# Attention stage of a fused attention and two-MoE kernel: scatters spread over chunks, state scaling on ScalarE, a product split over two engines, loads and fills in another order

## The chip, the cores and the metric

One core of a Trainium2 chip runs the whole kernel. The metric is device time in microseconds for one launch. Engines are named as in the profile: PE (TensorE), DVE (VectorE), ACT (ScalarE), POOL (GpSimd) and SP (SyncE, which here issues DMA transfers).

## The reference, cut to what matters

Three computations follow each other: an attention with a decaying state per head, a mixture of eight experts with one expert per token, and a second mixture that some tokens skip.

```python
# attention: B=4, H=8, S=768, D=48
for t in range(S):
    state = alpha[:, :, t, :, None] * state + einsum('bhd,bhe->bhde', k[:, :, t], v[:, :, t])
    y[:, :, t] = einsum('bhd,bhde->bhe', q[:, :, t], state)
x = y.transpose(0, 2, 1, 3).reshape(3072, 384)
# first MoE, E=8, F=1024: e_idx = argmax(x @ w_gate)
for e in range(E):
    out[mask] = gate_w[mask] * eom[mask, e] * (relu(x[mask] @ w1[e]) @ w2[e])
# second MoE: where x @ w_skip > 0, out = x + gate_w * (relu(x @ w1[e]) @ w2[e]); else out = x
```

## The kernel before

Attention works on 24 chunks of 128 time steps (4 batches of 6 chunks, all 8 heads at once as 4 pairs `hp`). Inside a chunk the decay is a running product `P` (`p_scan`, a DVE scan, L878). `p_recip` makes `r` = 1/P on ACT by a logarithm and an exponential. `p_k` makes `t` = P*r on POOL (L904), `r` = k*r on DVE (L911) and `k2` on DVE (L913). The product with t serves a Newton step. `p_q` makes `qp` = q*P on POOL (L922). PE multiplies k2 and qp (`scores`), DVE applies the causal mask to two tiles (`mask`, L941), PE transposes k2 (`k_back`), and ACT copies it out as `kn`. `state` has PE form `pu` from kn and v, and DVE adds the state of the chunk before (L976) and multiplies by the chunk's total decay `ptots` (L977; for the first chunk of a batch one instruction, L974). The last chunk of a batch needs no state. `y_of` forms y on PE; `x_rows` turns it into token rows.

The order is written out by hand. The list `stages` gives each step a lag, so that iteration i of the loop handles chunk i+4 in `p_scan`, chunk i+2 in `p_k` and `p_q`, chunk i in `scores` and `mask`, and chunk i-1 in `state` and `y_of`. Each engine executes its instructions in that program order. A declared dependency holds t back until the scan of the next chunk has ended. Every third iteration SP loads the next half batch of a, k, q (buffers for three halves) and one iteration later the v of a half (three buffers).

Four chunks (512 tokens) make a group. When its rows stand, `x_route` finds the expert of each token (iterations i%4==2 for groups 0 to 3), and one iteration later `x_place` computes the positions and issues four scatters, one per chunk, from POOL (L218) into `scr1`, a region of rows per expert in HBM. Group 4 is placed after the last mask but one, and group 5 is placed in the first expert's stage. `fill_region` (L139) writes empty rows to the head of each expert's region: `scr1` in two parts, of which the second comes at iteration 3, and `scr2` of the second mixture at iteration 16, all through SP. In iterations 7 to 23 with i%3 not 0, half a piece of expert 0's weights is split into a high and a low part (`split_half`, L303 on ACT and L304 on DVE).

After attention, `stream` runs 18 items: first expert 0 (306 rows, then 126 late rows), then experts 1 to 7 with 432 rows each, then the second mixture's experts. While one expert computes, the next expert's six weight pieces are loaded by SP (L292) through three buffers `st` and split. The rows of the first item use two of these buffers.

Of the kernel before, what the change touches and what calls it, by code (L numbers as in the profile page):

```python
# [8 lines left out]
F32 = mybir.dt.float32  # L9
# [4 lines left out]
AF = mybir.ActivationFunctionType  # L14
ALU = mybir.AluOpType
# [4 lines left out]
B, H, S, D = 4, 8, 768, 48  # L20
E, DM, FF = 8, 384, 1024
NT = B * S
C = 128
NCH = S // C
NTILE = NT // C
NP = H // 2
PR = 112
HB = 3
HALF = HB * C
CAP = 3456  # L30
# [7 lines left out]
P2, G2 = 128, 2  # L38
N2 = P2 * G2
GT = 4  # L40
LATE = 1
# [11 lines left out]
def kernel(  # L53
# [17 lines left out]
    nc = tc.nc  # L71
    ctx.enter_context(tc.manual_schedule())

    def pool(stack, name, bufs, space=None, **kw):
        if space is not None:
            kw["space"] = space
        return stack.enter_context(tc.tile_pool(name=name, bufs=bufs, **kw))
# [1 line left out]
    cp = pool(ctx, "const", 1)  # L79
    sp = pool(ctx, "small", 2)  # L80
    wpe = pool(ctx, "wpe", 1)
    rp = pool(ctx, "rows", 2)
    stp = pool(ctx, "stage", 3)
    psM = pool(ctx, "psM", 1, PSUM)
    dp = pool(ctx, "dram", 1, DRAM)
# [1 line left out]
    scr1 = dp.tile([E * CAP + N1, PAY], F32, name="scr1")  # L87
    scr2 = dp.tile([E * CAP + N1, PAY], F32, name="scr2")
# [7 lines left out]
    ecap = cp.tile([1, E], BF16, name="ecap")  # L96
    ecl1 = cp.tile([1, 2, E], BF16, name="ecl1")
# [8 lines left out]
    ptots = cp.tile([PR, NTILE, NP], F32, name="ptots")  # L106
# [30 lines left out]
    def fill_region(scr, pp, gg, e0=0, e1=E):  # L137
        for e in range(e0, e1):
            nc.sync.dma_start(  # L139
                out=scr[e * CAP:e * CAP + pp * gg, :].rearrange("(p g) d -> p g d", p=pp),  # L140
                in_=fill[0:pp, None, :].to_broadcast([pp, gg, PAY]),
            )
# [74 lines left out]
    def scatter(dst, idx, j, src, pp, bound, key=None):  # L217
        ins = nc.gpsimd.indirect_dma_start(  # L218
            out=dst, out_offset=bass.IndirectOffsetOnAxis(ap=idx.bitcast(U32)[0:pp, j:j + 1], axis=0),
            in_=src, in_offset=None, bounds_check=bound, oob_is_err=False,  # L220
        )
        if key is not None:
            if groups[key]:
                tc.declare_no_dep(ins.ins, group=key, reason="the rows differ")
            tc.add_to_no_dep_group(key, ins.ins)
            groups[key].append(ins)
# [19 lines left out]
        nc.vector.tensor_reduce(out=ls, in_=lo, axis=AX.X, op=ALU.add)  # L246
        return dl, ex, oh, ls

    def place_tokens(xrow, sm_ps, routed, row, key=None):
        dl, ex, oh, ls = routed  # L250
        psr = sm_ps[:, 256:256 + GT * E]
        rank_mm(128, GT, oh, ohs1, row, psr)
        em = sp.tile([128, GT], F32, name="em")
        nc.scalar.activation(out=em, in_=ls, func=AF.Exp, scale=-1.0)
        sm = exp_sum(128, GT, exps(128, GT, dl, "a") if ex is None else ex, "a")
        pos = sp.tile([128, GT], F32, name="posa")
        positions(128, GT, oh, psr, pos, "a")
        dn = sp.tile([128, GT], F32, name="dn")
        nc.vector.scalar_tensor_tensor(out=dn, in0=em, scalar=1.0, in1=sm, op0=ALU.add, op1=ALU.mult)
        pi = sp.tile([128, GT], I32, name="pi")  # L260
        nc.vector.tensor_copy(pi, pos)
        nc.vector.reciprocal(out=xrow[:, :, 384], in_=dn)
        count(128, GT, oh, ohs1, "a")
        for j in range(GT):
            scatter(scr1[:, :], pi, j, xrow[:, j, :], 128, E * CAP - 1, key)

    def rows_from(xt, pt):
        for hp in range(NP):
# [52 lines left out]
    def open_pools(stack, early=False):  # L321
        nonlocal wpo, mp, psH, psY, psT
        if not early:
            mp = pool(stack, "moe", 1, reuse_waits="tile")
        wpo = pool(stack, "wpo", 1, reuse_waits="tile")
        psH = pool(stack, "psH", 2, PSUM, reuse_waits="tile")
        psY = pool(stack, "psY", 3, PSUM, reuse_waits="tile")
        psT = pool(stack, "psT", 2, PSUM, reuse_waits="tile")
# [518 lines left out]
    with ExitStack() as actx:  # L847
        inp = pool(ictx, "inp", 1)
        wk = pool(actx, "wk", 2, side="right")
# [1 line left out]
        ps1 = pool(actx, "ps1", 1, PSUM)  # L851
        NB_IN = 3
        NQ = 4
        NB_V = 3
        ain = [inp.tile([128, HB, NP, C + 1], F32, name=f"ain{i}") for i in range(NB_IN)]
        kin = [inp.tile([128, HB, NP, C], F32, name=f"kin{i}") for i in range(NB_IN)]
        qin = [inp.tile([128, HB, NP, C], F32, name=f"qin{i}") for i in range(NB_IN)]
# [1 line left out]
        NHALF = 2 * B  # L859
# [7 lines left out]
        def load_v(h):  # L867
            b, u = divmod(h, 2)
            nc.sync.dma_start(out=vin[h % NB_V], in_=vn[b][:, u * HB:(u + 1) * HB])

        P_t, r_t, k_t, q_t, A_t, kn_t, S_t, x_t, xt_t, sm_t, rt_t, lt_t = ({} for _ in range(12))
        scans = {}

        def p_scan(i):
            h, c = divmod(i, HB)
            a = ain[h % NB_IN]
            P = wk.tile([PR, NP, C + 1], F32, name="P", bufs=4)
            scans[i] = nc.vector.tensor_tensor_scan(  # L878
                out=P.rearrange("p a b -> p (a b)"), data0=a[0:PR, c].rearrange("p a b -> p (a b)"),
                data1=floor[0:PR].rearrange("p a b -> p (a b)"), initial=1.0, op0=ALU.mult, op1=ALU.max,  # L880
            )
            P_t[i] = P[:, :, 1:C + 1]

# [34 lines left out]
        def p_q(i):  # L918
            h, c = divmod(i, HB)
            P = P_t[i]  # L920
            qp = wk.tile([PR, NP, C], F32, name="qp", bufs=NQ)
            nc.gpsimd.tensor_tensor(  # L922
                out=qp, in0=qin[h % NB_IN][0:PR, c], in1=P, op=ALU.mult
            )
            q_t[i] = qp
            nc.scalar.activation(out=ptots[:, i], in_=P[:, :, C - 1], func=AF.Copy)
# [34 lines left out]
        def state(i):  # L961
            b, c = divmod(i, NCH)
            if c == NCH - 1:
                return
            v, kn = v_of(i), kn_t.pop(i)
            pu = ps1.tile([PR, NP, D], F32, name="pu")
            for hp in range(NP):
                v0 = 2 * hp * D
                nc.tensor.matmul(pu[0:64, hp], kn[:, hp, 0:64], v[:, v0:v0 + D])
                nc.tensor.matmul(pu[64:PR, hp], kn[:, hp, 64:PR], v[:, v0 + D:v0 + 2 * D])  # L970
            sn = wk.tile([PR, NP, D], F32, name="S", bufs=3)
            pt = ptots[:, i, :, None].to_broadcast([PR, NP, D])
            if c == 0:
                nc.vector.tensor_tensor(out=sn, in0=pu, in1=pt, op=ALU.mult)  # L974
            else:
                nc.vector.tensor_tensor(out=sn, in0=pu, in1=S_t[i - 1], op=ALU.add)  # L976
                nc.vector.tensor_tensor(out=sn, in0=sn, in1=pt, op=ALU.mult)  # L977
            S_t[i] = sn

        def y_of(i):  # L980
# [56 lines left out]
        def x_place(i):  # L1037
            g, j = divmod(i, GT)
            if j == GT - 1:
                place_tokens(x_t.pop(g), sm_t[g], rt_t.pop(g), ecap if g < NTILE // GT - LATE else ecl1, "a")  # L1040

        def among(fn, i0, i1):
            def run(i):
# [6 lines left out]
        x_route_0, x_place_0 = (among(fn, 0, rest) for fn in (x_route, x_place))  # L1050
# [22 lines left out]
        for which, c in (("ak", 0), ("a", 1), ("q", 0), ("kq", 1), ("a", 2)):  # L1073
# [11 lines left out]
        pieces = []  # L1085
        stages = (
            (p_recip, 3), (scores, 0), (mask, 0), (state, -1), (x_route_1, -3), (p_k, 2), (p_q, 2), (k_back, 0),
            (x_place_0, -4), (x_place_1, -3), (x_route_0, -3), (p_scan, 4), (y_of, -1), (x_rows, -2), (p_check, 3),
        )

        def constants(n):
# [13 lines left out]
        for i in range(NTILE + 2):  # L1105
            if i == early_at + 1:
                bump(ohs1, ecl1, sm_t[NTILE // GT - LATE - 1][0:1, 400:401], EARLY1)
            for fn, lag in stages:
                if 0 <= i + lag < NTILE and (fn, i + lag) not in done:
                    fn(i + lag)  # L1110
                if fn is p_scan and 6 <= i < 24 and i % 3:
                    split_half(w_cur, (i - 6) // 3, i % 3 - 1, pieces[(i - 6) // 3])
            if i % HB == 1 and 2 <= (i + 2) // HB < NHALF:
                load_v((i + 2) // HB)
            if i == early_at:
                xe = []
                for g0 in range(0, ITEMS[0][4], 2):
                    g1 = min(g0 + 2, ITEMS[0][4])
                    st = stp.tile([128, 1024], F32, name="st")
                    part = st[:, 0:(g1 - g0) * PAY].rearrange("p (g d) -> p g d", g=g1 - g0)  # L1120
                    load_into(part, ITEMS[0], g0, g1)
                    xe += [part[:, g] for g in range(g1 - g0)]
            if i % HB == 0 and i // HB + 3 < NHALF:
                load_half(i // HB + 3, "akq")
            if i == HB:
                fill_region(scr1, P1, G1, FILL)
            if i == 16:
                fill_region(scr2, P2, G2)
            if 4 <= i and i % 3 == 1 and (i - 4) // 3 < 6:
                pieces.append(load_piece(w1a, w2a, 0, (i - 4) // 3, stp))  # L1130

# [59 lines left out]
            place_tokens(xrow, smp, route_tokens(smp), ecl1)  # L1191

    open_pools(ectx, early=True)
    last = NTILE - 1
    stream(w_cur, "b", "o", (xe, xc, x_first), {
        (0, 0): (lambda: x_route(last),), (0, 2): (lambda: x_place(last),),
# [97 lines left out]
```

## Time and profile before

| what | value |
|---|---|
| time before, median of 3 runs | 605.98 us (602.32 to 607.67) |
| the profiled execution's own time | 606.18 us |
| its span, first to last instruction | 604.5 us |
| PE busy | 558.1 us, 92% of the span |
| DVE busy | 385.7 us, 64% |
| ACT busy | 295.7 us, 49% |
| POOL busy | 179.0 us, 30% |
| mean granted TensorE clock | 0.948 |

The span is the time between the first and the last instruction that the profiler recorded. The busy shares are means over two very different stages, attention and experts.

### The profile page before, as it was taken

The numbers are of one execution on the slowest core, as the hardware profiler recorded it, in microseconds if no ns is written. First come the engines' busy times: TensorE is split into PE (matmuls) and PEld (weight loads), VectorE is DVE, ScalarE is ACT, GpSimd is POOL, SyncE is SP. The second block draws the span as 40 slices with busy tenths as digits, with TensorE's granted clock in tenths as the row PEclk, the third lists the DMA queues.
The fourth block names the chain that finished last, engine by engine and source line by source line (L and its number), as shares of the span: only waits on it lengthen the run. The fifth ranks groups of instructions, "written<-read, shape, count | busy, mean of one in ns | idle before, by whom it ended". The sixth has DMA issues, their size and how long they took to land.

```text
span 604.5 us, 11709 instructions
## 1 busy us (share of the span) xinstructions
PE 558.1 (92%) x4545; PEld 509.0 (84%) x4545; DVE 385.7 (64%) x872; ACT 295.7 (49%) x675; POOL 179.0 (30%) x186
## 2 busy tenths in 40 slices
PE   5895987979789999999999999999999999999995
PEld 3674875867569889999999999999998999999995
DVE  6798696979735546365555555463744777677751
ACT  4565463755334455353544444444544655555640
POOL 4155545455532032023140506060406010011111
PEclk9698878788888999999999999999999999999998
DMA  8999744960133822516171626253345567666620
GB/s 322 360 352 306 299 180 141 346 212 1 54 112 105 249 72 85 186 27 234 41 250 36 221 70 225 72 192 104 100 162 196 171 204 241 210 214 204 218 86 22
DMA packets 34797, 103.98 MB, mean 172 GB/s; under 512 B 6316, under 2 KB 13100, under 8 KB 34732
## 3 DMA queue, kind: packets, MB, share of 16 engines
q1 hardware_dynamic: 27788, 91.18, 45.0%
q0 software_dynamic: 6944, 11.96, 5.7%
q8 instruction: 38, 0.62, 0.5%
q14 instruction: 27, 0.22, 0.1%
HBM read 82.62 MB, written 27.13 MB: 182 GB/s over the span
## 4 chain that ended last, share of the span: by engine, by line
PE 67%; DVE 13%; DMA 10%; POOL 4%; SPq 2%; issue 2%; ACT 1%; POOLq 0%; DVEq 0%; ACTq 0%
PE ph L399 26%; PE py L446 16%; PE py L455 11%; DMA vin<-in_vn_dram 4%; PE py L399 3%; DVE r L911 3%; DVE A L941 3%; DVE P L878 2%; PE pt L355 2%; DMA st<-in_w2a_dram 2%; POOL scr L218 2%; PE pt L485 2%; DMA scr<-fill 2%; PE ph L417 2%; DVE k L913 1%
## 5 line engine op out<-in xcount | busy, mean ns | idle before, releaser
L218 POOL DMA_INDIRECT scr<-x,pi x56 | 67.8, 1210 | 218.9 <-DVE osb L201 133.3
L399 PE MATMUL ph<-xh,w1h 128*128 128x432 f32 (+3 forms) x330 | 110.1, 334 | 0.0
L399 PE MATMUL ph<-xl,w1h 128*128 128x432 f32 (+3 forms) x330 | 106.7, 323 | 0.0
L399 PE MATMUL ph<-xh,w1l 128*128 128x432 f32 (+3 forms) x330 | 106.5, 323 | 0.0
L405 DVE SCALAR_TENSOR_TENSOR hl<-ph,hh 128x432 fp32r<-128x432 f32 (+3 forms) x110 | 56.3, 512 | 69.3 <-ACT hh L404 68.4
L404 ACT ACTIVATE hh<-ph 128x432 fp32r<-128x432 f32 (+3 forms) x110 | 50.1, 455 | 91.0 <-PE ph L399 90.9
L304 DVE TENSOR_TENSOR w2l<-st,w2h 128x512 fp32r<-128x512 f32 x96 | 64.5, 688 | 41.0 <-ACT w2h L303 40.9
L303 ACT ACTIVATE w2h<-st 128x512 fp32r<-128x512 f32 x96 | 58.1, 625 | 47.0 <-DMA st<-in_w2a_dram 25.8
L446 PE MATMUL py<-hh,w2h 128*128 128x432 f32 (+1 forms) x192 | 69.1, 360 | 0.0
L446 PE MATMUL py<-hh,w2l 128*128 128x432 f32 (+1 forms) x192 | 67.5, 351 | 0.0
L446 PE MATMUL py<-hl,w2h 128*128 128x432 f32 (+1 forms) x192 | 67.4, 351 | 0.0
L304 DVE TENSOR_TENSOR w1l<-st,w1h 128x512 fp32r<-128x512 f32 x96 | 63.1, 686 | 4.4 <-ACT w1h L303 2.5
L399 PEld LDWEIGHTS ph<-xh,w1h 128*128 128x128 f32 x330 | 62.8, 190 | 2.7 <-issue 1.6
L399 PEld LDWEIGHTS ph<-xh,w1l 128*128 128x128 f32 x330 | 62.8, 190 | 1.1
L399 PEld LDWEIGHTS ph<-xl,w1h 128*128 128x128 f32 x330 | 62.5, 189 | 1.5
L934 PE MATMUL ps<-qp,k 48*128 48x128 f32 x384 | 37.7, 318 | 22.4 <-DVE A L941 13.5
L303 ACT ACTIVATE w1h<-st 128x512 fp32r<-128x512 f32 x96 | 56.5, 623 | 0.0
L934 PEld LDWEIGHTS ps<-qp,k 48*128 48x128 f32 x384 | 31.1, 215 | 28.3 <-issue 21.7
L218 POOL DMA_INDIRECT out_dram<-ot,ti x16 | 15.6, 976 | 119.6 <-DVE ot L550 109.2
L455 PE MATMUL py<-w2h,hh 128*128 128x384 f32 (+1 forms) x136 | 48.4, 356 | 0.0
L455 PE MATMUL py<-w2l,hh 128*128 128x384 f32 (+1 forms) x136 | 45.9, 337 | 0.0
L455 PE MATMUL py<-w2h,hl 128*128 128x384 f32 (+1 forms) x136 | 43.9, 337 | 0.0
(216 smaller groups left out, 1115.7 us busy)
## 6 DMA issues: line engine op xcount, KB each, us to landing
st<-in_w1a_dram SPq DMA_DIRECT2D x24, 512.0 KB
st<-in_w2a_dram SPq DMA_DIRECT2D x24, 512.0 KB
st<-in_w1b_dram SPq DMA_DIRECT2D x24, 512.0 KB
st<-in_w2b_dram SPq DMA_DIRECT2D x24, 512.0 KB
ain<-in_ad_dram SPq DMA_DIRECT2D x7, 774.0 KB
kin<-in_kd_dram SPq DMA_DIRECT2D x7, 768.0 KB
qin<-in_qd_dram SPq DMA_DIRECT2D x7, 768.0 KB
scr<-fill SPq DMA_DIRECT2D x8, 654.8 KB
```

The source lines that it names most:

```text
L218: ins = nc.gpsimd.indirect_dma_start(out=dst, out_offset=bass.IndirectOffsetOnAxis(ap=idx.bitcast(U32)[0:pp, j:j + 1], axis=0), in_=src, i ...
L303: nc.scalar.activation(out=hi, in_=src, func=AF.Copy)
L304: nc.vector.tensor_tensor(out=lo, in0=src, in1=hi.bitcast(F32), op=ALU.subtract)
L355: nc.tensor.transpose(pt[:, g * pp:(g + 1) * pp], rows_of(xr, g)[0:pp, kb * 128:(kb + 1) * 128], ident[0:pp, 0:pp])
L399: nc.tensor.matmul(ph[:, 0:n], w[:, kb, f * 128:(f + 1) * 128], x[:, kb, 0:n], start=(k == 0), stop=(k == 3 * KB - 1),)
L404: nc.scalar.activation(out=hh[:, f, 0:n], in_=ph[:, 0:n], func=AF.Relu)
L405: nc.vector.scalar_tensor_tensor(out=hl[:, f, 0:n], in0=ph[:, 0:n], scalar=0.0, in1=hh[:, f, 0:n].bitcast(F32), op0=ALU.max, op1=ALU.subtract,
L446: nc.tensor.matmul(py[d], w[:, f, dsl], hx[:, f, 0:pp * gg], start=(f == 0 and k == 0), stop=(f == FB - 1 and k == 2),)
L455: nc.tensor.matmul(py[g], hx[:, f, gsl], w[:, f, :], start=(f == 0 and k == 0), stop=(f == FB - 1 and k == 2),)
L911: nc.vector.tensor_tensor(out=r, in0=kk, in1=r, op=ALU.mult)
L934: nc.tensor.matmul(pss[j][:, hp], k2[rr, hp], qp[rr, hp])
L941: nc.vector.tensor_tensor(out=a, in0=ps, in1=causal[:, None, :].to_broadcast([128, NP, C]), op=ALU.mult)
```

## The change

Six things are changed in the attention stage. The scatters of groups 0 to 3 are collected in a list, and a new step `x_send`, right behind `x_place_0`, issues one of them per iteration; groups 4 and 5 still issue four in a row. The multiplication of the state by `ptots` goes from DVE to ACT, as one scaled copy per head pair (four per chunk). The product qp goes to DVE for chunks with i%4 of 2 or 3 and stays on POOL for the others. The v of a half is loaded at i%3==0 instead of 1, ahead of that iteration's a, k, q, with two buffers instead of three. The second part of scr1's fill is issued at iteration 0 instead of 3. The fill of scr2 is issued after the attention loop, ahead of the expert stage's loads. `P` has three buffers instead of four, and the token rows have three instead of two.

```diff
-    rp = pool(ctx, "rows", 2)
+    rp = pool(ctx, "rows", 3)
...
-    def place_tokens(xrow, sm_ps, routed, row, key=None):
+    def place_tokens(xrow, sm_ps, routed, row, key=None, later=None):
...
         for j in range(GT):
-            scatter(scr1[:, :], pi, j, xrow[:, j, :], 128, E * CAP - 1, key)
+            if later is None:
+                scatter(scr1[:, :], pi, j, xrow[:, j, :], 128, E * CAP - 1, key)
+            else:
+                later.append(lambda j=j: scatter(scr1[:, :], pi, j, xrow[:, j, :], 128, E * CAP - 1, key))
...
-        NB_V = 3
+        NB_V = 2
...
-            P = wk.tile([PR, NP, C + 1], F32, name="P", bufs=4)
+            P = wk.tile([PR, NP, C + 1], F32, name="P", bufs=3)
...
-            nc.gpsimd.tensor_tensor(
+            (nc.gpsimd if i < 2 or i % 4 < 2 else nc.vector).tensor_tensor(
                 out=qp, in0=qin[h % NB_IN][0:PR, c], in1=P, op=ALU.mult
             )
...
-            pt = ptots[:, i, :, None].to_broadcast([PR, NP, D])
-            if c == 0:
-                nc.vector.tensor_tensor(out=sn, in0=pu, in1=pt, op=ALU.mult)
-            else:
+            if c:
                 nc.vector.tensor_tensor(out=sn, in0=pu, in1=S_t[i - 1], op=ALU.add)
-                nc.vector.tensor_tensor(out=sn, in0=sn, in1=pt, op=ALU.mult)
+            for hp in range(NP):
+                nc.scalar.activation(
+                    out=sn[:, hp], in_=(sn if c else pu)[:, hp], func=AF.Copy, scale=ptots[:, i, hp:hp + 1]
+                )
...
+                    to_send if g < NTILE // GT - LATE - 1 else None,
...
+        def x_send(i):
+            if to_send:
+                to_send.pop(0)()
...
-            (x_place_0, -4), (x_place_1, -3), (x_route_0, -3), (p_scan, 4), (y_of, -1), (x_rows, -2), (p_check, 3),
+            (x_place_0, -4), (x_send, 0), (x_place_1, -3), (x_route_0, -3), (p_scan, 4), (y_of, -1), (x_rows, -2), (p_check, 3),
...
-            if i % HB == 1 and 2 <= (i + 2) // HB < NHALF:
-                load_v((i + 2) // HB)
...
+            if i % HB == 0 and NB_V <= i // HB + 1 < NHALF:
+                load_v(i // HB + 1)
             if i % HB == 0 and i // HB + 3 < NHALF:
                 load_half(i // HB + 3, "akq")
-            if i == HB:
+            if i == 0:
                 fill_region(scr1, P1, G1, FILL)
-            if i == 16:
-                fill_region(scr2, P2, G2)
...
     open_pools(ectx, early=True)
+    fill_region(scr2, P2, G2)
```

## Rows read from the trace of the kernel before

**Rows 1.** Windows: busy us and count per engine, granted clock, DMA share, GB/s.

```profile
190.00:600.00 410.00, 405.11 (x2661) 383.25 (x2660) 241.43 (x602) 200.94 (x428) 92.21 (x84) 1.00 0.47 152
81.70:88.30 6.60, 6.60 (x87) 5.40 (x87) 6.33 (x15) 4.11 (x11) 2.59 (x3) 0.79 0.92 383
132.00:137.50 5.50, 4.31 (x27) 3.77 (x29) 5.43 (x9) 3.72 (x11) 2.61 (x3) 0.53 0.01 3
```

**Rows 2.** Timeline of DVE: start, duration, instruction; one iteration, then part of the next.

```profile
44.94 1.23 DVE L878 TENSOR_TENSOR_SCAN P<-ain,floor 112x516 f32<-112x516 f32 x1
46.09 1.26 DVE L941 TENSOR_TENSOR A<-ps,causal 128x512 f32<-128x512 f32 x2
...
47.65 1.24 DVE L977 TENSOR_TENSOR S<-S,ptots 112x192 f32<-112x192 f32 x1
48.81 0.68 DVE L911 TENSOR_TENSOR r<-kin,r 112x512 f32<-112x512 f32 x1
...
50.13 1.23 DVE L878 TENSOR_TENSOR_SCAN P<-ain,floor 112x516 f32<-112x516 f32 x1
51.27 1.26 DVE L941 TENSOR_TENSOR A<-ps,causal 128x512 f32<-128x512 f32 x2
52.75 1.65 DVE L911 TENSOR_TENSOR r<-kin,r 112x512 f32<-112x512 f32 x1 [0.21 <-POOL t L904]
```

**Rows 3.** Timeline of DVE around a group's four scatters.

```profile
93.58 1.23 DVE L878 TENSOR_TENSOR_SCAN P<-ain,floor 112x516 f32<-112x516 f32 x1
94.73 0.67 DVE L304 TENSOR_TENSOR w1l<-st,w1h 128x512 fp32r<-128x512 f32 x1
...
101.39 1.66 DVE L911 TENSOR_TENSOR r<-kin,r 112x512 f32<-112x512 f32 x1 [4.80 <-POOL t L904]
...
128.33 1.66 DVE L911 TENSOR_TENSOR r<-kin,r 112x512 f32<-112x512 f32 x1 [3.02 <-POOL t L904]
```

**Rows 4.** Timeline of POOL in the same stretch.

```profile
76.26 1.46 POOL L904 TENSOR_TENSOR t<-P,r 112x512 f32<-112x512 f32 x1 [2.60 <-DVE P L878]
...
93.66 2.65 POOL L218 DMA_INDIRECT scr<-x,pi  x1 [2.72 <-DVE osa L201]
96.61 0.98 POOL L218 DMA_INDIRECT scr<-x,pi  x1 [0.30 <-DVE A L941]
...
100.16 1.19 POOL L904 TENSOR_TENSOR t<-P,r 112x512 f32<-112x512 f32 x1
```

**Rows 5.** DVE's waits, 0 to 185 us: total, times, longest.

```profile
DVE r L911 <- POOL t L904: 16.4, 5, 4.8
...
DVE S L974 <- PE pu L970: 2.8, 1, 2.8
```

**Rows 6.** Timeline of SP's DMA issues, 40 to 180 us.

```profile
40.01 8.10 SPq L139 DMA_DIRECT2D scr<-fill  x4
...
105.77 9.81 SPq L139 DMA_DIRECT2D scr<-fill  x8
...
175.14 0.68 SPq L336 DMA_DIRECT2D st<-scr  x2
175.93 8.01 SPq L292 DMA_DIRECT2D st<-in_w1a_dram  x3
```

**Rows 7.** Timeline of ACT: two short instructions, and expert 1's first split.

```profile
89.41 0.19 ACT L926 ACTIVATE ptots<-P 112x4 f32<-112x4 f32 x1
89.50 0.19 ACT L254 ACTIVATE em<-ls 128x4 f32<-128x4 f32 x1
...
193.46 0.63 ACT L303 ACTIVATE w1h<-st 128x512 fp32r<-128x512 f32 x1
```

**Rows 8.** Timeline of PE: two chunks' scores back to back, and scores after an idle stretch.

```profile
113.60 1.16 PE L934 MATMUL ps<-qp,k 48*128 48x128 f32 x16
...
118.72 1.16 PE L934 MATMUL ps<-qp,k 48*128 48x128 f32 x16
...
133.19 2.58 PE L934 MATMUL ps<-qp,k 48*128 48x128 f32 x16 [3.29 <-DVE A L941]
```

More of the change, by code (lines that the diff above doesn't have):

```diff
@@ L871 @@
         P_t, r_t, k_t, q_t, A_t, kn_t, S_t, x_t, xt_t, sm_t, rt_t, lt_t = ({} for _ in range(12))
-        scans = {}
+        scans, to_send = {}, []
         def p_scan(i):
@@ L1039, in x_place @@
             if j == GT - 1:
-                place_tokens(x_t.pop(g), sm_t[g], rt_t.pop(g), ecap if g < NTILE // GT - LATE else ecl1, "a")
+                place_tokens(
+                    x_t.pop(g), sm_t[g], rt_t.pop(g), ecap if g < NTILE // GT - LATE else ecl1, "a",
+                    to_send if g < NTILE // GT - LATE - 1 else None,
+                )
+        def x_send(i):
+            if to_send:
+                to_send.pop(0)()
         def among(fn, i0, i1):
```

## The prediction

> **What bounds the kernel now.** I read the stages first, as windows. From 190 to 600 us PE is busy for 405 of 410 us at granted clock 1.00 [rows 1]. The change issues almost nothing there. So what it can win lies in the attention stage, the first 185 us, where DVE is busy nearly throughout (6.33 of 6.60 us in one window [rows 1]), and whatever moves the end of that stage moves the end of the kernel by as much, because the experts start when attention's last rows are there.
>
> Inside attention I followed DVE in its timeline, from scan to scan. A plain iteration takes 5.19 us (44.94 to 50.13) without idle time: scan, two masks and the state's addition (46.09 to 47.65), its multiplication, r, k2 [rows 2]. Where a group has just been placed it is another thing: from the scan at 93.58 until r is done at 103.05 go 9.5 us, against 4.6 (44.94 to 49.49) in the plain one, because DVE waits 4.80 us for t [rows 2, 3]. POOL's timeline explains it: four scatters come one behind the other from 93.66, and t starts only at 100.16, though the scan that it must keep clear of ended at 94.8 [rows 3, 4]. DVE waited 16.4 us for t in five waits [rows 5]; 0.21 of them stand in rows 2, so 16.2 lie behind the four groups of scatters. One more stall is DVE's 2.8 us for pu [rows 5], at the first state of the third half: v comes late there, since SP issued it behind the second part of scr1's fill, which held SP for 8.10 us [rows 6].
>
> The sum is made against the profiled execution, 606.18 us with a span of 604.5; it lies 0.2 above the median of the runs, 605.98, so a difference carries over. About 1% (6 us) is what a measurement of this kernel can tell from no change.
>
> **Scatters, one per iteration.** A scatter behind the first costs POOL 0.98 plus 0.30, 1.28 us [rows 4]. Three of them leave the path ahead of t: 3.84 us per group, but no more than DVE waited, 3.02 at one of the four [rows 3]. Together 3 x 3.84 + 3.0 = 14.5 us. What is late next: the first scatter stays, 2.65 us long, so t starts at 96.6 instead of 95 and DVE still waits some 1 us. The 12 scatters that move land on POOL behind t or qp of later iterations, where POOL waited for the next scan anyway, for 2.60 us in a row of that kind [rows 4]. A scatter of 1.28 disappears in that; one that stretches like the first (2.65 + 0.30) exceeds it by 0.35. So the bounds are 13 (a third of those 12 pay 0.35) and 16 (all the waits of rows 5 go). I take 14.5.
>
> **State scaled by ACT.** This takes 1.16 us (47.65 to 48.81) off DVE in a plain iteration [rows 2]. That is not what is won. The iteration that follows in rows 2 has no state at all, yet from its masks until r is done it takes 3.13 us (51.27 to 54.40) against 3.40 (46.09 to 49.49): r now comes early, first waits for t and then runs beside qp on POOL, 1.65 us instead of 0.68. So where qp stays on POOL about 0.3 us is won per iteration. The Trainium skill's page "SBUF — State Buffer", section "Who interferes with whom", has a rule for it: a DVE instruction with two SBUF inputs contends with a GpSimd instruction that reads SBUF, and whichever issues second is blocked. By that rule the trace agrees (0.68 against 1.65 us); by durations alone the sum would hold 0.9 us more in each of some nine iterations, 8 us, which I do not count.
>
> **qp on DVE for half of the chunks.** There POOL reads nothing beside r. DVE loses the multiplication (up to 1.16) and gains qp, which is an instruction of r's form, 0.68 [rows 2]: 0.2 to 0.5 won. In the four iterations behind a placing r falls from 1.66 to 0.68 and qp is added: 0.3 won. With 20 iterations at 0.25 I count 5 us for these two parts, between 0 (PE cannot follow) and 9 (near 0.5 each).
>
> **What PE and ACT take back.** At a high clock two neighbouring chunks' scores are 5.12 us apart with PE busy throughout [rows 8], so PE doesn't let iterations fall much under 5 us. And its clock drops: after an idle stretch of 3.29 us the scores took 2.58 instead of 1.16 us, in a window granted 0.53, about the lower level of 1.2 GHz [rows 1, 8]. From r to r, two groups are 26.9 us apart before (101.39 to 128.33) [rows 3]; I expect 23. PE needs 20.5 for four chunks at clock 1.0 and 24 at 0.85. ACT gains four copies of 48 elements per chunk. The nearest rows are short instructions of 0.19 that follow each other every 0.09 us [rows 7], so 0.4 to 0.8 us per chunk. ACT was busy 4.11 us of 6.60 [rows 1]; 4.5 to 4.9 fit into a mean of 5.8, but hardly into a short iteration of 5. The copies wait on ACT for DVE's addition, and behind them wait kn, the weight split and the copy of y, which PE and DVE need an iteration later. I take 2 us back, between 0 and 6 (0.3 in each of 20 iterations).
>
> **v first, scr1's fill earlier.** The queue carries the same bytes up to there, but v of the third half now stands ahead of the fifth half's a, k, q: 2.3 MB, 6 us at the 383 GB/s of a window with a DMA share of 0.92 [rows 1]. So the stall of 2.8 us [rows 5] goes. Next in line are the first weight piece and the fifth half's a, which by the same rate land near the time at which a faster loop wants them. Bounds 0 and 2.8, taken 2. With two v buffers SP waits for y of a half's last chunk before it can issue the next v, and the loads of a, k, q queue behind that; in return v has four iterations, some 20 us, instead of three. The buffers of P and of the token rows add no wait: the buffer that a scan takes was read for the last time one iteration earlier, and a group's rows come round after 12 iterations.
>
> **scr2's fill at the border.** In its old place it held SP for 9.81 us [rows 6], at a time when no DVE wait is due to what stood behind it (the five of rows 5 are for t), so nothing is won there. In its new place it stands on SP behind the reads of the first expert's rows (175.14) and ahead of three weight pieces (175.93), which SP needed 8.01 us to issue because it waited for buffers [rows 6]. SP is past the fill at about 185.7; with 1.4 us for each piece of 0.52 MB at the rate above, they land at 188 to 191, and the first split begins at 193.46 [rows 7]. That is the cover: the part of expert 0 that comes ahead of the split. Without it up to 9.8 us are lost. I take 0.5, for the rows read beside the fill.
>
> **Sum.** 606.2 - 14.5 - 5 + 2 - 2 + 0.5 = 587.2; I predict 587.
>
> **Rivals.** First, everything is won: PE's clock stays up because its long idle stretches go, and the terms reach their good ends (16, 9, 0, 2.8, 0): 606.2 - 27.8 = 578. For it: the idle stretch of 3.29 us [rows 8] lies in the wait that the scatters caused. Against: PE's 5.12 us per chunk. Chance 0.13.
>
> Second, the fill at the border is bare: expert 1's weights come late and PE waits, 9.8 instead of 0.5: 596. For it: 9.81 us of SP time [rows 6]. Against: the cover above, of which 2 to 5 us are left over. Chance 0.10.
>
> Third, the slower side: ACT becomes the bound. As a mechanism of this kernel: an ACT iteration of 4.11 plus 0.8, to which the copies add a bare wait at the head of ACT's queue, for masks and addition (1.56 us) and in two of three iterations a weight split ahead of them (0.67) [rows 1 to 3]: 7.1 us, and every iteration follows it. The old mean is 26.9 / 4 = 6.7, so 20 iterations lose 8 us, less 2 for v: 612. It decides from an ACT iteration of 6.6 us on. Against it: logarithm and exponential run on ACT while DVE does the masks, so most of that wait is covered. Chance 0.04. A milder form (0.5 us in 8 short iterations) gives 591 and lies in the forecast. The Trainium skill's page "ScalarE: Activation LUTs", section "Rules for kernel authors", tells one to multiply on VectorE and to budget some 0.3 us per ACTIVATE. By it the four copies would be an estimated 1.4 us per chunk instead of 0.4 to 0.8; which of the two holds no run shows yet.
>
> Fourth, spreading doesn't do what it says: each scatter stretches to 2.65 us while DVE works and holds t up by 1 us in 12 iterations, so 12 of the 14.5 come back: 599. Chance 0.08.
>
> **How the numbers follow.** Forecast (582 to 593) 0.65; the rivals 0.13, 0.10, 0.04 and 0.08. The range reaches to the first and second rival, 578 to 597; it leaves out the slower one, the last and a part of the first, under 2 in 10. Faster by over 1% (under 600): the forecast, the first two and about half of the last, 0.92; within 1% 0.05; slower 0.03.
>
> **What would show it.** Right: POOL's timeline has single scatters between qp and t; DVE's wait for t falls from 16.4 to about 5 us; the wait for pu is gone; r still takes 1.65 where qp is on POOL; the expert stage begins near 166 us instead of 185 with no new wait of PE. Wrong: no idle time on ACT ahead of its logarithm; splits of expert 1 that wait for `st`; a granted clock under 0.8 throughout the loop; or group 4, still placed four in a row, waiting for a scatter queued ahead of it.

## The result and the profile after

| what | before | after |
|---|---|---|
| median (range) | 606.21 us (602.32 to 607.67) | 589.15 us (586.96 to 590.03) |
| ratio, 95% interval | | 0.9723 (0.9671 to 0.9775) |
| the profiled execution's own time, span | 606.18, 604.5 us | 590.03, 588.3 us |
| mean granted TensorE clock | 0.948 | 0.961 |
| first matmul of the experts (span start = 0) | 184.97 us | 166.38 us |
| from there to the end of the span | 419.5 us | 421.9 us |

587 was forecast, and 589.15 came. Lines of the changed kernel are numbered 3 higher (the scan is L881, t L907, r L914, qp L925, the state's addition L976), and the copies on ACT are L978. PE's timeline gives the experts' first matmul, in the kernel before and after:

```profile
184.97 0.62 PE L399 MATMUL ph<-xh,w1h 128*128 128x306 f32 x1
```

```profile
166.38 0.41 PE L402 MATMUL ph<-xh,w1h 128*128 128x306 f32 x1
```

The experts begin 18.6 us earlier and the span ends 16.2 us earlier. What is between, 2.4 us, was lost in the experts' own time; a second profile of the same kernel (below) loses only 0.8 of it, so most of it is no effect of the change.

DVE's timeline after, answering to [rows 2]: an iteration with qp on DVE, then the beginning of one with qp on POOL:

```profile
40.80 1.23 DVE L881 TENSOR_TENSOR_SCAN P<-ain,floor 112x516 f32<-112x516 f32 x1
...
43.12 0.35 DVE L976 TENSOR_TENSOR S<-pu,S 112x192 f32<-112x192 f32 x1
43.42 0.69 DVE L914 TENSOR_TENSOR r<-kin,r 112x512 f32<-112x512 f32 x1
...
44.75 0.68 DVE L925 TENSOR_TENSOR qp<-qin,P 112x512 f32<-112x512 f32 x1
45.35 1.23 DVE L881 TENSOR_TENSOR_SCAN P<-ain,floor 112x516 f32<-112x516 f32 x1
...
52.52 1.66 DVE L914 TENSOR_TENSOR r<-kin,r 112x512 f32<-112x512 f32 x1 [0.21 <-POOL t L907]
```

The plain iteration falls from 5.19 to 4.55 us, and r is 1.66 where qp is on POOL and 0.69 where it is not. The stretch behind a placing, answering to [rows 3], on DVE and then on POOL [rows 4]:

```profile
86.32 1.23 DVE L881 TENSOR_TENSOR_SCAN P<-ain,floor 112x516 f32<-112x516 f32 x1
87.46 0.67 DVE L307 TENSOR_TENSOR w1l<-st,w1h 128x512 fp32r<-128x512 f32 x1
...
90.28 0.69 DVE L914 TENSOR_TENSOR r<-kin,r 112x512 f32<-112x512 f32 x1 [0.95 <-POOL t L907]
```

```profile
86.39 2.64 POOL L218 DMA_INDIRECT scr<-x,pi  x1 [2.46 <-DVE osa L201]
89.06 1.19 POOL L907 TENSOR_TENSOR t<-P,r 112x512 f32<-112x512 f32 x1
90.42 1.44 POOL L218 DMA_INDIRECT scr<-x,pi  x1 [0.17 <-issue]
93.62 1.18 POOL L907 TENSOR_TENSOR t<-P,r 112x512 f32<-112x512 f32 x1 [1.77 <-DVE P L881]
94.97 1.45 POOL L218 DMA_INDIRECT scr<-x,pi  x1 [0.16 <-issue]
```

From the scan until r is done go 4.65 us, against 9.5. One scatter stands ahead of t, and the others end before the scan that the next t waits for. DVE's waits, 0 to 185 us, answering to [rows 5] (total, times, longest):

```profile
DVE A L944 <- PE ps L937: 7.8, 4, 3.3
...
DVE r L914 <- POOL t L907: 5.2, 9, 1.1
```

Waiting for t fell from 16.4 to 5.2 us, and the line for pu is gone. What is longest now is DVE's wait for the scores `ps` of PE. In the kernel before it was less than half of that:

```profile
DVE A L941 <- PE ps L934: 3.4, 3, 2.0
```

Of the 7.8 us, 3.2 lie before 26 us, while the loop starts, and 4.6 at its end. Windows show what the engines do there (busy time per engine, granted clock, DMA share, GB/s):

```profile
39.80:45.40 5.60, 5.16 (x83) 4.28 (x85) 5.53 (x10) 5.12 (x15) 1.19 (x1) 1.00 0.79 277
133.00:139.00 6.00, 4.81 (x58) 3.79 (x53) 5.24 (x11) 4.05 (x13) 5.47 (x4) 0.81 0.09 33
139.00:145.00 6.00, 6.00 (x72) 4.89 (x73) 4.18 (x8) 3.83 (x14) 4.00 (x3) 0.62 0.28 101
151.00:158.00 7.00, 7.00 (x71) 5.92 (x72) 2.47 (x8) 1.79 (x6) 4.35 (x5) 0.56 0.31 117
```

In the first row DVE, PE and ACT are all nearly full (5.53, 5.16 and 5.12 of 5.60 us) at clock 1.00: the short iteration leaves no engine much room. In the last two rows PE is busy throughout at 0.62 and 0.56, near the lower of its two levels (1.2 GHz). Ahead of that, in the second row, it was busy for 4.81 of 6.00 us, and one idle stretch of 1.00 us stands in front of the scores. PE's timeline and DVE's there, answering to [rows 8]:

```profile
135.79 2.20 PE L937 MATMUL ps<-qp,k 48*128 48x128 f32 x16 [1.00 <-DVE A L944]
145.29 1.16 PE L937 MATMUL ps<-qp,k 48*128 48x128 f32 x16
```

```profile
146.49 1.29 DVE L944 TENSOR_TENSOR A<-ps,causal 128x512 f32<-128x512 f32 x2 [3.27 <-PE ps L937]
```

Two neighbouring chunks' scores are 9.5 us apart, and that mask is the one behind which group 4 is routed, placed and sent. What these waits cost at the experts' start is taken up with the order of the loads, below: less than they last.

### The profile page after: what moved, and what is told of

Its sections match the earlier page's. It is cut to its first block, busy times and chain, and to the rows that moved or that the text cites. A ratio compares the mean times of both kernels' runs of the same rounds, so it can differ in the third digit from the quotient of the medians.

```text
span 588.3 us, 11764 instructions
## 1 busy us (share of the span) xinstructions
PE 554.5 (94%) x4545; PEld 503.9 (86%) x4545; DVE 377.7 (64%) x864; ACT 313.6 (53%) x755; POOL 169.9 (29%) x174
## 5 line engine op out<-in xcount | busy, mean ns | idle before, releaser
L218 POOL DMA_INDIRECT scr<-x,pi x56 | 72.3, 1291 | 215.7 <-DVE ski L533 91.4
L937 PE MATMUL ps<-qp,k 48*128 48x128 f32 x384 | 36.4, 321 | 13.0 <-DVE k L916 7.7
```

Of the source, the lines that this page charges most:

```text
L218: ins = nc.gpsimd.indirect_dma_start(out=dst, out_offset=bass.IndirectOffsetOnAxis(ap=idx.bitcast(U32)[0:pp, j:j + 1], axis=0), in_=src, i ...
L937: nc.tensor.matmul(pss[j][:, hp], k2[rr, hp], qp[rr, hp])
```

## The experiments

Each ratio is to the kernel before, run in turn with it on the same chip (medians of before: 607.72 us beside the first four, 609.62 beside the next four, 605.26 beside the last four). The ratio is taken over the runs in turn and lies up to 0.3% beside the quotient of the two medians. "Start" is the experts' first matmul in the profile.

| run | median, us | ratio (95%) | start, us |
|---|---|---|---|
| e1_scatter | 596.10 | 0.9787 (0.9743 to 0.9831) | 170.33 |
| e2_state | 605.93 | 0.9965 (0.9936 to 0.9994) | 183.23 |
| e3_qp | 609.53 | 1.0004 (0.9970 to 1.0039) | 184.33 |
| e4_loads | 606.05 | 0.9942 (0.9914 to 0.9969) | 183.08 |
| e5_four | 604.83 | 0.9925 (0.9901 to 0.9950) | 176.87 |
| e6_fill16 | 592.96 | 0.9723 (0.9694 to 0.9752) | 165.84 |
| e7_qp_dve | 592.75 | 0.9722 (0.9684 to 0.9760) | 163.96 |
| e10_scatter_loads | 596.93 | 0.9797 (0.9769 to 0.9825) | 170.93 |
| after_again | 587.97 | 0.9728 (0.9698 to 0.9758) | 165.82 |
| e8_qp_pool | 586.95 | 0.9708 (0.9681 to 0.9735) | 167.07 |
| e9_vmul | 590.51 | 0.9767 (0.9739 to 0.9795) | 166.78 |
| e11_route_first | 583.15 | 0.9632 (0.9602 to 0.9661) | 161.25 |

**One part alone, on the kernel before.** e1_scatter has the list, `x_send` and the three changed buffer counts:

```diff
+                    to_send if g < NTILE // GT - LATE - 1 else None,
...
+            (x_place_0, -4), (x_send, 0), (x_place_1, -3), (x_route_0, -3), (p_scan, 4), (y_of, -1), (x_rows, -2), (p_check, 3),
```

> The kernel before with the scatters of groups 0 to 3 spread, one per iteration, and the buffers that this needs (three of token rows, three of P, two of v), nothing else. My theory (the prediction's first term): 14.5 us off, so about 591.5, with DVE's wait for t in the attention stage falling from 16.4 to about 5 us. Rival (a stretched scatter holds t in later iterations): 2 to 5 us off, 601 to 604, with single scatters of 2.6 us and POOL without idle time ahead of t.

It starts the experts 14.6 us earlier and is worth 2.1%: 13 us by the ratio, 11.6 by the medians. DVE's waits, 0 to 185 us, show what it leaves:

```profile
DVE A L944 <- PE ps L937: 5.8, 5, 1.5
DVE S L977 <- PE pu L973: 3.5, 1, 3.5
```

Between 40 and 150 us its waits for t are down to 1.2 us in all; the wait for pu, which belongs to the loads, stays.

e2_state has the copies on ACT alone:

```diff
-                nc.vector.tensor_tensor(out=sn, in0=sn, in1=pt, op=ALU.mult)
+            for hp in range(NP):
+                nc.scalar.activation(
+                    out=sn[:, hp], in_=(sn if c else pu)[:, hp], func=AF.Copy, scale=ptots[:, i, hp:hp + 1])
```

> The kernel before with the state scaled on ACT alone. My theory: r moves up and then runs beside qp on POOL, 1.66 instead of 0.68 us, so only some 0.3 us per plain iteration is won, 4 us in all, 602; ACT's four copies take 1.0 us, as in the kernel after, and cost nothing. Rival A (durations count): 0.9 to 1.2 us in each of 16 iterations, 14 to 18 us off, 588 to 592. Rival B (ACT's added microsecond is on the path): 0 to 10 us slower.

It is 0.35% faster, 2.1 us. Its DVE timeline, one plain iteration:

```profile
44.95 1.23 DVE L878 TENSOR_TENSOR_SCAN P<-ain,floor 112x516 f32<-112x516 f32 x1
47.09 1.29 DVE L941 TENSOR_TENSOR A<-ps,causal 128x512 f32<-128x512 f32 x2 [0.92 <-PE ps L934]
48.30 0.35 DVE L973 TENSOR_TENSOR S<-pu,S 112x192 f32<-112x192 f32 x1
48.56 0.68 DVE L911 TENSOR_TENSOR r<-kin,r 112x512 f32<-112x512 f32 x1
49.28 0.69 DVE L913 SCALAR_TENSOR_TENSOR k<-t,r 112x512 f32<-112x512 f32 x1
49.89 1.23 DVE L878 TENSOR_TENSOR_SCAN P<-ain,floor 112x516 f32<-112x516 f32 x1
```

4.94 us from scan to scan instead of 5.19: here DVE's freed time goes into a wait of 0.92 for PE's scores, and r takes 0.68. In the iteration before it (scans at 40.05 and 44.95) there is no wait, and the time goes into r beside POOL's qp, as expected:

```profile
42.66 1.65 DVE L911 TENSOR_TENSOR r<-kin,r 112x512 f32<-112x512 f32 x1
```

And with four scatters still together, what was won before a placing is waited away there: DVE's waits for t are 19.7 us in eight, against 16.4.

e3_qp has the split of qp alone:

```diff
-            nc.gpsimd.tensor_tensor(
+            (nc.gpsimd if i < 2 or i % 4 < 2 else nc.vector).tensor_tensor(
```

> The kernel before with qp of half the chunks on DVE alone. My theory: POOL reads less beside DVE, so the state's multiplication falls from 0.9 to 1.24 to under 0.7 us and r behind the scatters from 1.66 to 0.68, which pays for the 0.65 of qp: 0 to 3 us off, 603 to 606. Rival (DVE is the bound and gains work): 0.65 us in each of 11 chunks, 7 us slower, 613.

Nothing measurable (0.997 to 1.0039). A plain iteration with qp on DVE takes 4.91 us there (scans at 45.44 and 50.35), and the multiplication of the state stands in it with its own price:

```profile
48.15 0.36 DVE L977 TENSOR_TENSOR S<-S,ptots 112x192 f32<-112x192 f32 x1
```

Against 1.24 us beside qp [rows 2]. So of the 1.16 us that I took off DVE for it, 0.8 was the price of running beside POOL's qp. By the Trainium skill, page "SBUF — State Buffer", section "Who interferes with whom", a DVE instruction with two SBUF inputs contends with a GpSimd instruction that reads SBUF; the trace agrees, for r (0.69 and 1.66) and for this one (0.36 and 1.24).

e4_loads has the order of v, the two fills and `NB_V` alone:

```diff
-            if i == HB:
+            if i == 0:
                 fill_region(scr1, P1, G1, FILL)
...
+            if i % HB == 0 and NB_V <= i // HB + 1 < NHALF:
+                load_v(i // HB + 1)
```

> The kernel before with the transfers alone reordered: v first with two buffers, second part of scr1's fill at iteration 0, scr2's fill behind attention. My theory: the stall of 2.8 us for pu goes and up to 1 us comes back at the border (the kernel after waits 4.1 us on ACT for the first weight pieces, then catches up), so 1 to 2 us off, 604 to 605. Rival (the fill is bare at the border): 4 to 10 us slower, 610 to 616, with PE idle after the first expert.

0.58% faster by the ratio, 3.5 us; the medians differ by 1.7 and the experts' start by 1.9. The wait for pu is gone.

**Parts taken out of the changed kernel, or put on top of each other.** e5_four issues the four scatters at once again:

```diff
-                    to_send if g < NTILE // GT - LATE - 1 else None,
+                    None,
```

> The kernel after with the four scatters of each group issued at once again, all else as after. My theory: the waits behind the scatters come back whole, 13 to 15 us, so 602 to 604, ratio to before near 0.995. Rival (the other parts now hide them, since r no longer meets qp there): 3 to 8 us back, 592 to 597.

Of the 2.8% only 0.75% is left. Its DVE timeline behind a placing, to be set beside 90.28 above:

```profile
88.53 1.23 DVE L881 TENSOR_TENSOR_SCAN P<-ain,floor 112x516 f32<-112x516 f32 x1
...
96.34 0.69 DVE L914 TENSOR_TENSOR r<-kin,r 112x512 f32<-112x512 f32 x1 [4.80 <-POOL t L907]
```

Everything else of the change is in it, and the wait of 4.80 us is back to the hundredth.

e6_fill16 puts scr2's fill back at iteration 16:

```diff
+            if i == 16:
+                fill_region(scr2, P2, G2)
...
-    fill_region(scr2, P2, G2)
```

> The kernel after with scr2's fill issued at iteration 16 again. My theory (the fill at the border is covered but for a microsecond): 588 to 589, no difference that can be told; ACT's wait of 4.1 us for the first weight pieces goes, but PE waits there in neither kernel. Rival (bare fill): 4 us or more faster, 585.

The same ratio as the change, 0.9723. The fill's place costs nothing that can be measured. The reason is not that the weights come in time behind it: ACT's timeline of the changed kernel shows a wait for them at expert 1's first split [rows 7]:

```profile
176.65 0.63 ACT L306 ACTIVATE w1h<-st 128x512 fp32r<-128x512 f32 x1 [2.57 <-DMA st<-in_w1a_dram]
```

ACT waits there, but PE's one wait for ACT in that stretch is 1.59 us (1.7 in e6_fill16, 1.5 in the kernel before).

e10_scatter_loads is e1_scatter plus e4_loads, with qp and the state as before:

```diff
+                    to_send if g < NTILE // GT - LATE - 1 else None,
...
+            if i % HB == 0 and NB_V <= i // HB + 1 < NHALF:
+                load_v(i // HB + 1)
...
+            if i == 0:
                 fill_region(scr1, P1, G1, FILL)
...
+    fill_region(scr2, P2, G2)
```

> Spread scatters and reordered transfers together, with the state multiplied on DVE and qp on POOL as before. My theory (scatters 13, transfers 2 to 3 off, state and qp worth 2 to 3 of the gain): 591 to 592. Rival A (state and qp are worth nothing): 589. Rival B (the spread scatters need a POOL without qp to disappear): 596 or more.

No better than e1_scatter (0.9797 and 0.9787), though the wait for pu is gone and the last scan starts 2.5 us earlier (137.22 against 139.74). The lead is lost behind that scan: group 4's first scatter starts at 154.51 against 155.35, and SP can read the first expert's rows only at 163.16 against 162.43. PE's windows over the last scores of e10_scatter_loads are at a lower clock:

```profile
139.00:145.00 6.00, 5.17 (x52) 4.30 (x52) 5.93 (x9) 4.06 (x12) 5.18 (x5) 0.72 0.18 66
151.00:157.00 6.00, 3.92 (x38) 3.27 (x37) 3.79 (x20) 1.39 (x4) 2.18 (x2) 0.54 0.07 28
```

In e1_scatter the same two windows are granted 1.00 and 0.86. (Between them, 145 to 151 us, both kernels have 1.00; behind them, 157 to 163, they have 0.61 and 0.57.)

e7_qp_dve and e8_qp_pool take qp to one engine, DVE (from chunk 2 on) in the one:

```diff
-            (nc.gpsimd if i < 2 or i % 4 < 2 else nc.vector).tensor_tensor(
+            (nc.gpsimd if i < 2 else nc.vector).tensor_tensor(
```

and in e8_qp_pool

```diff
-            (nc.gpsimd if i < 2 or i % 4 < 2 else nc.vector).tensor_tensor(
+            nc.gpsimd.tensor_tensor(
```

> The kernel after with qp of all chunks from 2 on on DVE. My theory: where qp was on POOL, r falls from 1.36 to 1.66 us to 0.69 and qp adds 0.61, so 0 to 0.35 us per iteration are won in nine iterations, unless PE's 5.1 us per chunk takes it: 587 to 589. Rival (DVE is the bound and gains work): 0.3 to 0.6 us lost in each of nine, 592 to 595.

> The kernel after with qp of every chunk on POOL, all else as after. My theory: with the state on ACT the split is worth 0.3 us or more in each of some ten iterations, because r meets no qp there; 2 to 4 us slower than after, first expert matmul near 169. Rival (the split is worth nothing, as alone, where it changed the time by less than could be told): as after.

Groups of lines, DVE's r between 30 and 160 us (busy us, mean ns, idle before), in e7_qp_dve and then in e8_qp_pool:

```profile
L914 DVE TENSOR_TENSOR r<-kin,r 112x512 f32<-112x512 f32 x20 | 13.7, 687 | 5.0 <-POOL t L907 5.0
```

```profile
L914 DVE TENSOR_TENSOR r<-kin,r 112x512 f32<-112x512 f32 x20 | 31.3, 1566 | 5.1 <-POOL t L907 5.1
```

The collision is as expected, 0.88 us per r, and the experts start at 163.96, 165.82 (after_again, below) and 167.07 us with all, half and none of qp on DVE. But the three ratios, 0.9722, 0.9728 and 0.9708, can't be told apart. I expected e8_qp_pool to be slower by 2 to 4 us; that fell. Where its lag of 1.25 us at the start went was not isolated: its experts take 417.6 us, those of after_again 420.3.

after_again is the changed kernel once more, beside e8, e9 and e11.

> The kernel after once more, unchanged, beside the three that follow, for the spread from chip to chip: ratio to before 0.970 to 0.976, first matmul of the experts between 165 and 168 us (166.4 in its first profile).

Both came as expected; the experts start 0.6 us earlier than in the first profile.

e9_vmul is the changed kernel with the state multiplied on DVE:

```diff
-            for hp in range(NP):
-                nc.scalar.activation(
-                    out=sn[:, hp], in_=(sn if c else pu)[:, hp], func=AF.Copy, scale=ptots[:, i, hp:hp + 1])
+                nc.vector.tensor_tensor(out=sn, in0=sn, in1=pt, op=ALU.mult)
```

> The kernel after with the state's multiplication on DVE, all else as after. My theory: 0.4 to 0.9 us more in iterations where qp is on DVE and up to 0.3 in the others; 4 to 6 us slower than after, first expert matmul 170 to 172. Rival A (ACT's copies cost what they save): as after or faster. Rival B (the state is worth what it was alone): 1 to 2 us slower.

Its median is 2.5 us above that of after_again, with intervals that overlap (0.9739 to 0.9795, 0.9698 to 0.9758), and its experts start 1.0 us later: less than the 4 to 6 us that I expected. Its DVE timeline tells why, once with qp on DVE and once with qp on POOL:

```profile
42.62 0.36 DVE L980 TENSOR_TENSOR S<-S,ptots 112x192 f32<-112x192 f32 x1
...
83.97 0.91 DVE L980 TENSOR_TENSOR S<-S,ptots 112x192 f32<-112x192 f32 x1
84.80 0.68 DVE L914 TENSOR_TENSOR r<-kin,r 112x512 f32<-112x512 f32 x1
```

Beside POOL's qp the multiplication and r share one collision: in the second pair the multiplication pays it and r goes free.

**A better version.** All of qp on DVE does not show in the time, I thought, because the end of the loop is set by PE's scores and by what DVE does between the last mask but one and group 4's scatters. e11_route_first is e7_qp_dve with group 4's routing, placing and scatters ahead of the scores and the mask of iteration 22:

```diff
+        x_send_0, x_send_1 = among(x_send, 0, rest + 6), among(x_send, rest + 6, NTILE)
...
-            (p_recip, 3), (scores, 0), (mask, 0), (state, -1), (x_route_1, -3), (p_k, 2), (p_q, 2), (k_back, 0),
-            (x_place_0, -4), (x_send, 0), (x_place_1, -3), (x_route_0, -3), (p_scan, 4), (y_of, -1), (x_rows, -2), (p_check, 3),
+            (x_route_1, -3), (x_send_1, 0), (x_place_1, -3),
+            (p_recip, 3), (scores, 0), (mask, 0), (state, -1), (p_k, 2), (p_q, 2), (k_back, 0),
+            (x_place_0, -4), (x_send_0, 0), (x_route_0, -3), (p_scan, 4), (y_of, -1), (x_rows, -2), (p_check, 3),
```

> The kernel with qp on DVE from chunk 2 on, and in iteration 22 the routing and placing of group 4 ahead of scores and masks, so that DVE doesn't wait for PE's scores before it routes. My theory: at the end of attention the path runs through PE's late scores, the masks, the routing and the scatters; the scatters of group 4 start 2 us earlier and the first expert matmul comes at 161 to 163 instead of 164; 2 to 4 us faster than after, 585 to 587. Rival A (the path there is PE's own work, which keeps its length): as after. Rival B (the weight loads of the first experts set the time): first expert matmul earlier, total as after.

583.15 us, ratio 0.9632: 4.8 us under after_again in the median, its interval clear of that of after_again, and more than the 2 to 4 expected. The first scatter of group 4 on POOL's timeline, in e11_route_first and then in the changed kernel's first profile:

```profile
145.12 0.99 POOL L218 DMA_INDIRECT scr<-x,pi  x1 [3.67 <-DVE osa L201]
```

```profile
150.72 1.48 POOL L218 DMA_INDIRECT scr<-x,pi  x1 [7.25 <-DVE osa L201]
```

It comes 5.6 us earlier, and the experts start 5.1 us earlier (161.25 against 166.38). Part of this is e7_qp_dve's, on which it is built: beside that kernel the scatter comes 1.4 us earlier (146.52 there) and the experts start 2.7 us earlier (163.96), while the ratio falls from 0.9722 to 0.9632.

## Why the prediction was right

**The place was right.** The time came out of attention alone. From the sixth scan to the last the changed kernel needs 17.0 us less (29.57 to 148.81 before, 30.97 to 133.24 after); from there to the experts 3.0 us less; the sixth scan came 1.4 later and the experts took 2.4 longer (in after_again 0.1 and 0.8). The experts began near 166, as written.

**Scatters, 14.5 taken.** Shown: 14.6 us at the experts' start and 12 to 13 in the time for this part alone (e1_scatter). Taken out of the whole change it gives 11 at the start and 12 in the time (e5_four against e6_fill16 on the same chip, which is the change but for a fill that costs nothing). DVE's waits for t differ by 15.1 us between e5_four and the change, so some 4 us of them do not reach the experts' start. Where these go was not settled: DVE's waits for PE's scores are 5.0 us in e5_four and 7.8 in the change, but 10.1 in after_again and 5.4 in e6_fill16. The moved scatters took 1.01 to 1.45 us and disappeared in POOL's waits for the next scan (in the last group, which has no next scan, t once follows a scatter without idle time, at 138.80), so the fourth rival, that they stretch and hold t up, did not come about.

**State and split, 5 taken together, less 2 for PE and ACT.** The net, 3, was somewhat small: from e10_scatter_loads to after_again it is 4.2 us in the time (0.9797 to 0.9728, on two chips) and 5.1 at the experts' start. The shares were not seen rightly. With the copies, a plain iteration gains 0.28 us where qp stays on POOL (4.91 from scan to scan in e8_qp_pool), as the 0.3 of the prediction; with both parts it gains 0.64, above the 0.2 to 0.5, as long as PE's lead lasts (below). On the kernel before, the split alone is worth nothing (e3_qp) and the copies 2.1 us (e2_state). On top of the spread scatters and the loads, four kernels show each part with and without the other:

| on top of scatters and loads | ratio | start, us |
|---|---|---|
| neither (e10_scatter_loads) | 0.9797 | 170.93 |
| split alone (e9_vmul) | 0.9767 | 166.78 |
| copies alone (e8_qp_pool) | 0.9708 | 167.07 |
| both (after_again) | 0.9728 | 165.82 |

At the experts' start either part alone gives 3.9 to 4.2 of the 5.1 us, and the second adds 1.0 to 1.3. In the time the copies alone give 5.4 us, with intervals that lie apart; the split alone (1.8 us) and what one part adds to the other lie within theirs. The step that failed is the price of 1.16 us for the multiplication: 0.36 is its own, and 0.80 is the collision with qp, which either part removes, or hands on to r. So most of what was to come off DVE was qp's share, and the two parts are in the main two ways to the same gain.

**PE's and ACT's take-back.** In the changed kernel PE's came at the end of the loop, as waits for scores of up to 3.27 us at clock 0.62, and not as 0.3 in each iteration. That PE doesn't let iterations fall much under 5 us held. Behind the scans 4.55 us apart, PE's scores are 5.25 us apart at clock 1.00:

```profile
43.88 1.16 PE L937 MATMUL ps<-qp,k 48*128 48x128 f32 x16
49.13 1.16 PE L937 MATMUL ps<-qp,k 48*128 48x128 f32 x16
```

PE lives on a lead there: from the end of a chunk's scores to the start of its masks go 2.4, 1.5 and 0.8 us in three iterations. In after_again, whose granted clock is 0.79 from 40 to 50 us, the lead is gone an iteration earlier, DVE waits, and the scans are 4.55 and then 5.53 us apart:

```profile
46.18 1.29 DVE L944 TENSOR_TENSOR A<-ps,causal 128x512 f32<-128x512 f32 x2 [0.90 <-PE ps L937]
```

ACT's four copies were estimated at 0.4 to 0.8 us and took 1.01. The group of lines, 30 to 160 us:

```profile
L978 ACT ACTIVATE S<-S,ptots 112x48 f32<-112x48 f32 x64 | 16.2, 323 | 12.0 <-DVE S L976 11.7
```

One lasts 0.32 us, and since they overlap, 16.2 us for 64 make 0.25 each. Four in a row take the 1.01. The Trainium skill's page "ScalarE: Activation LUTs", section "Rules for kernel authors", gives some 0.3 us per ACTIVATE: the trace agrees on one, while the estimate of 1.4 us for four, which I worked out from it as four single times, is too much. The advice of that page of the Trainium skill, to multiply on VectorE, shows no gain here (e9_vmul, 2.5 us above in the median). ACT did wait for DVE's addition, 11.7 us in 12 waits, yet the loop became shorter, so the third rival fell. It came nearer than I thought: ACT's waits for the scan, ahead of the logarithm, were more than halved between 30 and 150 us, before and after:

```profile
ACT r L887 <- DVE P L878: 42.7, 17, 6.7
```

```profile
ACT r L890 <- DVE P L881: 17.0, 13, 2.7
```

**v first, 2 taken.** The stall went, and alone that gives 1.9 at the start and 1.7 to 3.5 us in the time (e4_loads). On top of the scatters it gives nothing that can be measured (e10_scatter_loads against e1_scatter). That the loss there comes of the lower clock in the last iterations fits the windows, but was not tested by itself, and two things speak against it as the whole cause. From the last scan to the experts e10_scatter_loads takes 3.1 us more than e1_scatter (33.7 and 30.6). Of these, 1.6 pass while SP waits for the transfers of the last scatter, 3.3 us from its end on POOL against 1.7. And e6_fill16, the changed kernel but for the fill, has the windows from 133 to 157 us at clock 1.00, waits of 1.16 us at most for the last scores, and group 4's first scatter at 149.20, 1.5 us ahead of the changed kernel; still its experts start at 165.84, and those of after_again at 165.82. PE's timeline, at the first expert's rows, in e6_fill16 and then in the changed kernel:

```profile
161.51 0.60 PE L358 MATMUL ps<-ident,st 102*128 102x102 f32 x2 [2.44 <-DMA st<-scr]
```

```profile
163.19 0.39 PE L358 MATMUL ps<-ident,st 102*128 102x102 f32 x2 [0.34 <-DMA st<-scr]
```

In e6_fill16 PE is done earlier, idles for 2.44 us and goes on at a granted clock of 0.50 (161.5 to 166 us); in the changed kernel it idles for 0.34 and 1.02 us and goes on at 1.00 (163 to 166.4). What PE saved in the last iterations it lost again in front of the experts. So the first rival, in which a clock that stays up wins the rest, fell too: between the last scan and the experts the two kernels differ by 1.1 us.

**The fill at the border, 0.5 taken.** It costs nothing that can be measured (e6_fill16). The cover that I named did not hold: the pieces were late by 2.6 us for expert 1's first split, one of the signs by which I would have known that I was wrong. What covered them was that ACT's splits are themselves ahead of PE's need (PE shows no wait for them), so the second rival fell for another reason than I gave.

Added up at the experts' start, 19.0 us were forecast and 18.6 came. Scatters and loads together gave 14.0 (e10_scatter_loads), 2.5 less than forecast, since the 2 us for v did not add up. From there to the change it is 4.6 us (170.93 to 166.38), where 3 less 0.5 for the fill were forecast, 2.1 too little. The second figure is what is left of the whole, and so no check on it. That the two errors cancel is luck.

## What to carry to other kernels

When one engine's queue mixes long bookkeeping with work that another engine waits for, find the wait behind the batch and spread the batch over the iterations; that was about three quarters of this gain in the time. A duration read beside another engine's instruction can hold that engine's share: look for the same instruction in a stretch where the neighbour is idle before taking it off the path. And parts that each show a gain alone need not add up: the loads gave some 2 us alone and nothing on top of the scatters, and the copies and the split remove one and the same collision. What ends the stage wants a look of its own: the order of the last group, with all of qp on DVE, gave as much again (4.8 us) as copies and split together.

## What the runs showed of the hardware

The same DVE multiplication of 112x192 took 0.36 us with POOL free of t and qp, 1.24 beside a qp begun 0.16 us before it [rows 2], 0.91 beside one begun 0.49 us before it (e9_vmul, 83.97), 1.02 beside t (e9_vmul, 65.50) and 2.16 beside t and qp in a row (e10_scatter_loads, 65.55). The first scatter of a group took 2.64 us where DVE had a scan, a weight split and masks beside it (86.39 and 133.31 in the changed kernel), 1.99 without the split (110.20), and single ones behind t or qp took 1.01 to 1.45. PE's first matmul of the experts took 0.62 us in e6_fill16, at a granted clock of 0.50 behind an idle stretch of 2.44 us, and 0.41 in the changed kernel, at 1.00. The experts, whose code the variants leave alone, took 419.5 to 422.7 us in the profiles of before, e1_scatter, e2_state, e4_loads and the change, 417.6 to 422.1 in the last four runs of the table, and 423.3 to 427.2 in the four runs beside a before of 609.62, so times are compared as ratios within one chip.
